# Reordering the state's fading, the next decay's mask and one weighing of scores in an mLSTM cell followed by a gated feed-forward block

## The chip, the cores and the metric

The kernel runs on one core of one Trainium2 chip. A core has five engines that run their own instruction streams in order and meet only at semaphores: TensorE (PE in the profile, with its weight loads shown apart as PEld), VectorE (DVE), ScalarE (ACT), GpSimd (POOL) and SyncE (SP, which here only issues DMAs). The metric is device time in microseconds (us) for one execution; lower is better. All arithmetic is float32, except for a few warm-up matmuls and the first two cells' masks.

## The reference, cut to what matters

An mLSTM cell (4 batches, 8 heads, 768 steps, head size 40) feeds a gated feed-forward block (3072 tokens, 320 features, 2048 hidden units).

```python
for t in range(S):
    m_new = np.maximum(f_gate[:, :, t] + m, i_gate[:, :, t])
    f_stab = np.exp(f_gate[:, :, t] + m - m_new)
    i_stab = np.exp(i_gate[:, :, t] - m_new)
    m = m_new
    C = f_stab * C + i_stab * outer(vt, kt)
    n = f_stab * n + i_stab * kt
    h_tilde = C @ qt
    denom = max(abs(n . qt), 1.0)
    y[:, :, t] = sigmoid(o_gate[:, :, t]) * h_tilde / denom
x = y.transpose(0, 2, 1, 3).reshape(B * S, H * D)
h = x @ w_in
out = (h * cos(h)) @ w_out
```

The two weight matrices arrive as 64-bit floats and are rounded to 32 bits inside the kernel.

## The kernel before, in words

**Cells.** The recurrence is done in chunks of 128 steps. There are six chunks (`c`) and four batches (`b`), so N = 24 cells, numbered n = 4c + b; B is 4. For one cell, `scores(n)` (L530, PE) makes the products of keys and queries of the 8 heads in two PSUM tiles `ps`, even heads and odd heads. `decay_exponents(n)` (L434, POOL) puts the causal mask on the tile `E`, which a DMA has filled; for n below 4 a DVE subtraction comes ahead of the mask, and for n from 4 on the mask is all of it. `decay(n)` (L448, ACT, eight instructions) exponentiates `E`. `weigh(n)` (L536, DVE, two instructions) multiplies `E` by the scores. `values(n)` (L556 to L565, PE) makes the cell's output `vt` from `E` and from the state carried over from the chunk ahead. `seam(n)` (L667, PE) makes the increment of the state in the PSUM tile `pu`. `fade(n)` (L650, POOL, four instructions) multiplies the state `st` by the chunk's decay, once `values(n)` has read it, and `state(n)` (L692, DVE, four instructions) adds `pu` to it. `denominators(n)` and `divide(n)` (L583 to L604, DVE) turn `vt` into `xT`, the input of the feed-forward block. `scale_q` (L512) and `weigh_k` (L453), on POOL, prepare the next cell's queries and keys. The four tiles `ps`, `ps`, `vt` and `pu` of one cell take turns in two PSUM buffers: the second score tile of a cell takes the buffer of the last cell's `pu`, and so can only be written when `state` of the last cell has read it.

**Feed-forward.** For chunk c and pair f2 of 128-wide column blocks, `Up(c, f2)` (L709 and L715, PE) makes two PSUM tiles `pup` of 512 tokens. Then `near` (L723, ACT) rounds to whole turns, `rest` (L726, DVE) makes the remainder, `sin` (L731, ACT) takes the sine, and `gate` (L735, DVE) multiplies it by `pup`, which gives `g`. There are two `pup` buffers, so the next `Up` starts when `gate` has read them. `down(c, f2)` (L829, PE, 16 matmuls in chunk 0) multiplies `g` by two blocks of `w_out`.

**Rounding of weights.** A piece of a weight matrix is loaded as 64-bit words (`bits`, `blocks`). `take_apart` (L167, L169) runs on ACT, `bound` and `join` (L173, L174, L183) on DVE, `round_up` (L187) on POOL. `on_vector` writes out the last three for a list of pieces. `down(0, 1)` reads the second piece of `w_out`.

**Order.** The schedule is written by hand: each engine runs its instructions in the order in which the program issues them, and the framework adds the semaphores. `first_cells` does cells 0 to 3, `first_period` does cell 4 beside `Up(0, 0)` and `Up(0, 1)`, and then `both_parts(c, b)` does cell 4(c+1) + b beside two `Up`s each, with i = 0 and i = 1; `both_parts(0, 1)` with i = 0 has `Up(0, 2)` and cell 5. In chunk 0 the weights are still being loaded and rounded. The SP queue issues nearly all loads; in `first_period` its last ones are `load_G(6)`, `load_two(6)`, `load_out` (which waits for a `bits` buffer that an earlier `round_up` has read) and `load_M(7)`.

Of the kernel before, what the change touches and what calls it, by code (L numbers as in the profile page):

```python
# [29 lines left out]
def kernel(  # L30
# [158 lines left out]
    def on_vector(made):  # L189

        for dst, bits in made:
            bound(dst)
        for dst, bits in (*made[1:], *made[0:1]):
            join(dst, bits)
        for dst, bits in made:
            round_up(dst, bits)
# [225 lines left out]
    def psum_o():  # L422
        return ps_o.tile([128, HP, C], FP, name="pm", tag="o")
# [6 lines left out]
    def decay_exponents(n):  # L430
        E = Es[n]
        if n < B:
            nc.vector.tensor_tensor(out=E, in0=E, in1=cols(n, 0, C), op=OP.subtract)
        nc.gpsimd.affine_select(out=E, in_=E, compare_op=OP.is_ge, fill=1.0e30, base=0,  # L434
                                pattern=[[0, H], [1, C]], channel_multiplier=-1)
# [140 lines left out]
    def denominators(n):  # L576

        K = C // 32
        if n == B:
            d = p2.tile([128, K, 32], FP, name="dt", tag="dt")  # L580
        else:
            d = heads_of[n][:, 3].rearrange("q (k i) -> q k i", k=K)
        nc.vector.transpose(out=d, in_=heads_of[n][:, 2].rearrange("q (t k) -> q k t", t=32))  # L583
        dn = dns[n] = p2.tile([128, K, 2], FP, name="d2", tag="d2")
        both = d[:, :, FROM0:FROM1 + 1:FROM1 - FROM0]
        nc.vector.scalar_tensor_tensor(out=dn, in0=both, scalar=-TWO_PI, in1=least.rearrange("q (k g) -> q k g", g=2), op0=OP.mult, op1=OP.max)
        nc.vector.scalar_tensor_tensor(out=dn, in0=both, scalar=TWO_PI, in1=dn, op0=OP.mult, op1=OP.max)
        if n > B:
            dns[n] = d[:, :, 0:2]
        nc.vector.reciprocal(out=dns[n], in_=dn)  # L590
# [53 lines left out]
    def fade(n):  # L644

        if B <= n < N - B:
            c, b = divmod(n, B)
            for j, r, s, w in halves(n):
                d = tab[r, c, 3, ts(b, H)].rearrange("p (a j) -> p a j", j=2)[:, :, j]
                nc.gpsimd.tensor_tensor(out=s, in0=s, in1=d.unsqueeze(2).to_broadcast([D, HP, w.stop - w.start]), op=OP.mult)  # L650
# [548 lines left out]
    def first_period():  # L1199
        n = B  # L1200
        up = Up(0, 0)
        scores(n)
        warm(8, psum_o())
        for e in range(2):
            up.near(e)
        for e in range(2):
            up.rest(e)
        weigh(n)
        for e in range(2):
            up.sin(e)  # L1210
            up.gate(e)
        values(n)
        seam(n)
        p, piece = outs.pop(0)
        take_apart(*piece)
        low_dimensions(n + 1)
        for some in pieces:
            take_apart(*some)
        out_of_psum(n)
        on_vector([piece])  # L1220
        up = Up(0, 1)
        turn_blocks(n + 1)
        on_vector(pieces)
        pieces.clear()
        more = weights_in(2)
        pieces.append(next(more))
        load_M(n + 2)
        pieces.extend(more)
        load_blocks(n + 2)
        load_out(p)  # L1230
        for e in range(2):
            up.near(e)
        for e in range(2):
            up.rest(e)
        for e in range(2):
            up.sin(e)
            up.gate(e)
        p, piece = outs.pop(0)
        take_apart(*piece)
        denominators(n)  # L1240
        on_vector([piece])
        fade(n)
        state(n)
        decay_exponents(n + 1)
        odd_values_of(n + 1)
        down_slot(0, 1)
        sigmoid(1)
        decay(n + 1)
        divide(n)
        scale_q(n + 1)  # L1250
        weigh_k(n + 1)
        load_G(n + 2)
        load_two(n + 2)
        load_out(p)
        load_M(n + 3)
# [6 lines left out]
    def both_parts(c, b):  # L1262

        n = (c + 1) * B + b
        cell = n < N
        for i in range(2):
            f2 = 2 * b + i
            up = Up(c, f2)
            if cell and i == 0:
                scores(n)  # L1270
            if cell and i == 1:
                if n % 2 == 1 and n > B + 1 and n + 3 < N:
                    load_two(n + 3)
            for e in range(2):
                up.near(e)
            for e in range(2):
                up.rest(e)
            if i == 0:
                if cell:
                    weigh(n)  # L1280
                    if n + 1 < N:
                        decay_exponents(n + 1)
                for e in range(2):
                    up.sin(e)
                    up.gate(e)
                if (c, b) == (0, 1):
                    seam_out(B)
                if c > 0:
                    sums(c, f2)
                if b == 0 and c == 1:  # L1290
                    sigmoid(c + 1)

                if c == 0:
                    p, piece = outs.pop(0)
                    made = [piece, *(pieces.pop(0) for _ in range(min(2 if b < 2 else 3, len(pieces))))]
                    for dst, bits in made:
                        take_apart(dst, bits)
                    on_vector(made[0:2])
                    load_out(p)
                    if b + 2 < B:  # L1300
                        load_blocks(n + 2)
                    if n in (B + 1, B + 2):
                        low_dimensions(n + 1)
                if c > 0 and cell and n + 1 < N:
                    decay(n + 1)
            else:
                if cell:
                    seam_out(n)
                if cell:
                    state(n)  # L1310
                for e in range(2):
                    up.sin(e)
                    up.gate(e)
                if c > 0:
                    sums(c, f2)
                if c == 0:
                    p, piece = outs.pop(0)
                    made = [*([pieces.pop(0)] if b == 1 else ()), piece]
                    for dst, bits in made:
                        take_apart(dst, bits)  # L1320
                    decay(n + 1)
                    sin_next()
                    on_vector(made[0:-1])
                    turn_blocks(n + 1, "k")
                    on_vector(made[-1:])
                if cell and n + 1 < N:
                    if c > 0:
                        weigh_k(n + 1)
                    odd_values(n + 1)
            down_slot(c, f2)  # L1330
            if cell and i == 0:
                values(n)
                seam(n)
                normalize_turned(n)
                fade(n)
                if c == 1 and b < 3:
                    weight_sums(b + 1)
                if n > B + 1 and n + 2 < N:
                    load_blocks(n + 2)
                if n > B + 1 and n + 3 < N:  # L1340
                    load_E(n + 3)
                if b == B - 2 and c + 2 < NC:
                    load_o(c + 2)
                if c == 0:
                    on_vector(made[2:])
                    if b + 2 < B:
                        pieces.extend(weights_in(b + 2))
                if c > 0:
                    sin_next()
            if i == 1:  # L1350
                if c == 0 and b + 2 < B:
                    load_two((n + 3) // 2 * 2)
                    load_E(n + 3)
                if c == 0:
                    turn_blocks(n + 1, "q")
                    scale_q(n + 1)
                    weigh_k(n + 1)
                    load_out(p)
                elif cell and n + 1 < N:
                    turn_blocks(n + 1)  # L1360
                    if n + 1 < (fast + 1) * B:
                        scale_q(n + 1)
                if b == B - 1 and c == fast - 1:
                    sigmoid(c + 2)
                if (c, f2) == (0, LAST):
                    weight_sums(0)
                if c == fast - 1 and b > 0:
                    up_weight_sums(b - 1)
                if c == fast - 1 and b == B - 1:
                    x_sums(c + 1)  # L1370
# [139 lines left out]
```

## Time and profile before

| what | value |
|---|---|
| median of 3 runs | 516.61 us (516.18 to 516.68) |
| profiled execution | 517.38 us, of it span from first to last instruction 515.5 us |
| busy PE | 499.2 us (97% of the span) |
| busy DVE | 417.7 us (81%) |
| busy ACT | 326.4 us (63%) |
| busy POOL | 300.9 us (58%) |
| moved by DMA | 57.87 MB, mean 112 GB/s |
| granted TensorE clock | 0.999 of full speed |

Times in the trace count from the span's start. A line of the timeline has start, duration, engine, line of the kernel, operation, output and inputs, how many instructions were merged into it, and in brackets the time that the engine stood idle ahead of it and what released it. "PE ps L530 <- DVE st L692" in the view of waits means that PE waited, ahead of an instruction of line 530 that writes `ps`, for an instruction of DVE of line 692 that writes `st`.

The period that the diff touches lies between about 56 and 74 us. In the slices from 56 to 64 us the sixteen DMA engines are busy all the time (mean share 1.02 to 1.05), and in most slices up to 130 us over 0.8.

### The profile page before, as it was taken

Reading aid. Unit: us, or ns where it says so; the run is one execution under the profiler, and the core shown is the slowest. Engines: PE = TensorE matmul, PEld = TensorE weight load, DVE = VectorE, ACT = ScalarE, POOL = GpSimd, SP = SyncE. Lnnn points to the kernel's source line nnn. Section 1 sums busy time; section 2 is a strip of 40 time slices with the busy share of each in tenths; the row PEclk is TensorE's granted clock in tenths of the full one; section 3 lists DMA queues with packets and bytes.
Section 4 is the critical chain, followed back from the end, with each engine's and each line's share of the span. In section 5 each row is a group of like instructions: output and inputs, shape, how many; then the busy total and the mean of one; then the engine's idle time right before and its main releaser. Section 6 shows DMA issues by size and latency. Waiting matters only on the chain.

```text
span 515.5 us, 11095 instructions
## 1 busy us (share of the span) xinstructions
PE 499.2 (97%) x4038; PEld 377.1 (73%) x4038; DVE 417.7 (81%) x839; ACT 326.4 (63%) x618; POOL 300.9 (58%) x387
## 2 busy tenths in 40 slices
PE   6999898999999999999999999999999999999997
PEld 3874454655666677778878778878878878687876
DVE  4799788988778888789987989988979867677655
ACT  2889787685945547748658867557867554443541
POOL 7525556553934855858566869656768454535340
PEclk9999999999999999999999999999999999999999
DMA  9979989998167337305728204937202000010001
GB/s 136 217 194 250 261 184 270 184 229 170 27 193 144 117 85 139 93 32 167 178 71 163 71 31 143 190 85 160 72 32 79 7 6 4 3 53 0 1 0 53
DMA packets 100903, 57.87 MB, mean 112 GB/s; under 512 B 63520, under 2 KB 93312, under 8 KB 100848
## 3 DMA queue, kind: packets, MB, share of 16 engines
q1 hardware_dynamic: 97696, 55.48, 45.9%
q10 hardware_dynamic: 2752, 1.23, 0.9%
q8 instruction: 32, 0.52, 0.4%
q0 software_dynamic: 400, 0.44, 0.3%
q14 instruction: 23, 0.19, 0.1%
HBM read 51.71 MB, written 4.11 MB: 108 GB/s over the span
## 4 chain that ended last, share of the span: by engine, by line
PE 72%; DVE 8%; DMA 6%; POOL 4%; ACT 3%; issue 3%; SPq 3%; DVEq 0%; POOLq 0%; ACTq 0%
PE acc L979 23%; PE pup L783 16%; PE pup L715 6%; PE pup L799 6%; PE late L979 4%; PE ps L530 3%; PE po L829 3%; DMA G<-G_d 2%; PE pup L709 2%; DMA blocks<-in_moe_w_in_dram 2%; PE vt L565 2%; DMA qr<-in_q_dram 2%; PE vt L556 2%; DVE t L508 1%; PE pw L1061 1%
## 5 line engine op out<-in xcount | busy, mean ns | idle before, releaser
L723 ACT ACTIVATE n<-pup 128x512 int32<-128x512 f32 x64 | 37.0, 594 | 97.6 <-DVE pup L808 65.0
L731 ACT ACTIVATE n<-n 128x512 f32<-128x512 f32 x96 | 58.2, 627 | 21.6 <-DVE n L726 15.9
L818 POOL TENSOR_TENSOR g<-g,n 128x512 f32<-128x512 f32 x31 | 39.5, 1276 | 51.4 <-ACT n L731 47.3
L726 DVE SCALAR_TENSOR_TENSOR n<-pup,n 128x512 f32<-128x512 f32 x64 | 43.1, 689 | 22.3 <-ACT n L723 19.7
L715 PE MATMUL pup<-xT,w_in_sb 128*128 128x512 f32 x128 | 58.8, 602 | 1.9 <-DVE g L735 1.7
L979 PE MATMUL acc<-w_out_sb,g 128*128 128x160 f32 x320 | 58.4, 302 | 0.0
L800 POOL TENSOR_TENSOR blocks<-blocks 128x256 f32<-128x256 f32 x32 | 25.6, 799 | 53.2 <-ACT blocks L792 53.1
L979 PE MATMUL acc<-T,g 128*128 128x160 f32 x304 | 55.8, 301 | 0.0
L448 ACT ACTIVATE E<-E,tab 128x128 f32<-128x128 f32 x160 | 50.2, 391 | 5.6 <-POOL E L434 5.4
L783 PE MATMUL pup<-xT,w_in_sb 128*128 128x256 f32 x192 | 53.1, 385 | 0.3 <-ACT blocks L792 0.2
L979 PEld LDWEIGHTS acc<-w_out_sb,g 128*128 128x128 f32 x320 | 48.9, 190 | 4.5 <-issue 2.7
L735 DVE TENSOR_TENSOR g<-pup,n 128x512 f32<-128x512 f32 x64 | 42.6, 687 | 6.1 <-ACT n L731 5.6
L715 PEld LDWEIGHTS pup<-xT,w_in_sb 128*128 128x128 f32 x128 | 23.0, 189 | 33.0 <-issue 31.2
L979 PEld LDWEIGHTS acc<-T,g 128*128 128x128 f32 x304 | 46.1, 190 | 0.9 <-issue 0.4
L783 PEld LDWEIGHTS pup<-xT,w_in_sb 128*128 128x128 f32 x192 | 33.8, 189 | 9.6 <-ACT blocks L792 5.9
L808 DVE TENSOR_TENSOR pup<-pup,blocks 128x256 f32<-128x256 f32 x32 | 13.9, 435 | 30.7 <-PE pup L799 27.5
L783 PE MATMUL pup<-x_room,room 128*128 128x256 f32 x128 | 38.2, 380 | 0.0
L791 ACT COPY blocks<-pup 128x512 f32<-128x512 f32 x32 | 18.6, 581 | 29.6 <-PE pup L783 27.8
L829 PE MATMUL po<-w_out_sb,g 128*128 128x320 f32 x128 | 36.3, 436 | 0.1
L979 PE MATMUL acc<-T,blocks 128*128 128x160 f32 x160 | 36.2, 308 | 0.0
L799 PE MATMUL pup<-xL,w_in_l 64*128 64x512 f32 x128 | 36.1, 641 | 0.0
L512 POOL TENSOR_TENSOR qG<-t,G 128x512 f32<-128x512 f32 x20 | 25.9, 1296 | 17.1 <-DVE t L508 16.9
(214 smaller groups left out, 1220.4 us busy)
## 6 DMA issues: line engine op xcount, KB each, us to landing
E<-M_d SPq DMA_DIRECT2D x21, 512.0 KB
qr<-in_q_dram SPq DMA_DIRECT2D x72, 80.0 KB
kr<-in_k_dram SPq DMA_DIRECT2D x72, 80.0 KB
bits<-in_moe_w_out_dram SPq DMA_DIRECT2D x8, 640.0 KB
G<-G_d SPq DMA_DIRECT2D x18, 256.0 KB
blocks<-in_moe_w_in_dram SPq DMA_DIRECT2D x32, 128.0 KB
out_dram<-o_sb SPq DMA_DIRECT2D x23, 160.0 KB
o<-in_o_gate_dram SPq DMA_DIRECT2D x40, 80.0 KB
```

The source lines that it names most:

```text
L448: nc.scalar.activation(out=Es[n][:, h], in_=Es[n][:, h], func=AF.Exp, scale=-1.0, bias=tab[:, c, 0, g:g + 1])
L512: nc.gpsimd.tensor_tensor(out=qG, in0=qkT[n][0], in1=Gs[n], op=OP.mult)
L715: nc.tensor.matmul(pu.rearrange("p (b t) -> p b t", b=B), w_in_sb[:, i, ts(2 * f2 + e, 128)], xT[c][:, i:NK * B:NK], start=(i == 0 and not ...
L723: nc.scalar.activation(out=self.n[e], in_=self.pu[e], func=AF.Copy, bias=0.25)
L726: nc.vector.scalar_tensor_tensor(out=self.n[e].bitcast(FP), in0=self.pu[e], scalar=0.25, in1=self.n[e], op0=OP.add, op1=OP.subtract)
L731: nc.scalar.activation(out=r, in_=r, func=AF.Sin, scale=TWO_PI_DOWN)
L735: nc.vector.tensor_tensor(out=g, in0=self.pu[e], in1=self.n[e].bitcast(FP), op=OP.mult)
L783: nc.tensor.matmul(bank[:, part].rearrange("p (b t) -> p b t", b=B // 2), w[:, f2], x, start=start, stop=stop, skip_group_check=True)
L799: nc.tensor.matmul(pu, w_in_l[r, f2], xL[c][r].rearrange("p b t -> p (b t)"), start=False, stop=True, skip_group_check=True)
L818: tt(out=self.g, in0=self.g, in1=self.n[e].bitcast(FP), op=OP.mult)
L829: nc.tensor.matmul(po[c][b], gs[c, f][:, ts(b, C)], w_out_sb[:, f], start=(f == 0), stop=(f == NF - 1))
L979: nc.tensor.matmul(a, lhs, rhs, start=start, stop=stop)
```

## The change

In `first_period`, `fade(4)` and `decay_exponents(5)` are issued ahead of `on_vector([piece])`, where piece is the second of `w_out`. On POOL the order was round_up, fade, mask, and becomes fade, mask, round_up. On DVE the order stays, since `fade` and the mask (for cells from 4 on) have no DVE instruction: bound, join, state as before. On PE, ACT and SP nothing moves.

In `both_parts`, for c = 0 and f2 = 2 alone (cell 5), `weigh` is issued ahead of `near` and `rest`. On DVE the order was rest, rest, weigh, weigh, and becomes weigh, weigh, rest, rest. On the other engines nothing moves.

```diff
@@ -1238,10 +1238,10 @@
         p, piece = outs.pop(0)
         take_apart(*piece)
         denominators(n)
+        fade(n)
+        decay_exponents(n + 1)
         on_vector([piece])
-        fade(n)
         state(n)
-        decay_exponents(n + 1)
         odd_values_of(n + 1)
         down_slot(0, 1)
         sigmoid(1)
@@ -1271,13 +1271,16 @@
             if cell and i == 1:
                 if n % 2 == 1 and n > B + 1 and n + 3 < N:
                     load_two(n + 3)
+            if (c, f2) == (0, 2):
+                weigh(n)
             for e in range(2):
                 up.near(e)
             for e in range(2):
                 up.rest(e)
             if i == 0:
                 if cell:
-                    weigh(n)
+                    if (c, f2) != (0, 2):
+                        weigh(n)
                     if n + 1 < N:
                         decay_exponents(n + 1)
                 for e in range(2):
```

## The prediction

> **What bounds the kernel now.** I read the page first, for the engine that can't be spared. PE is busy 97% of the span, so the end moves only if PE's idle time does. The second view is the list of what PE waited for over the whole run.
>
> ```profile
> PE   6999898999999999999999999999999999999997
> PE pw L1061 <- DVE room L1064: 4.0, 1, 4.0
> PE ps L530 <- DVE st L692: 1.9, 1, 1.9
> PE pup L783 <- ACT blocks L791: 1.8, 5, 0.8
> PE pup L715 <- DVE g L735: 1.7, 2, 1.4
> PE ps L530 <- DVE t L508: 1.6, 2, 1.1
> ```
>
> Columns of the lower five: total us, times, longest. The wait on `st` is the one that the diff can touch. PE's timeline between 61 and 106 us shows where the rest of the idle time lies that depends on it (idle time in brackets):
>
> ```profile
> 61.99 0.38 PE L530 MATMUL ps<-t,t 40*128 40x128 f32 x2
> 64.23 1.16 PE L530 MATMUL ps<-t,t 40*128 40x128 f32 x14 [1.86 <-DVE st L692]
> 83.11 3.67 PE L715 MATMUL pup<-xT,w_in_sb 128*128 128x512 f32 x8 [1.39 <-DVE g L735]
> 105.48 3.67 PE L715 MATMUL pup<-xT,w_in_sb 128*128 128x512 f32 x8 [0.32 <-DVE g L735]
> ```
>
> After 105.48 only about 3 us of PE waits are left in 410, all for work of the same stage, so what PE has gained by 105.48 it keeps to the end. But PE waits again at 83.11 for `gate` of Up(0, 3): in this stage DVE and ACT are the slower chain, and what counts is how much earlier *they* get there. So third, the timelines of POOL, DVE and ACT around the change.
>
> ```profile
> 57.93 0.75 POOL L187 TENSOR_TENSOR w_in_l<-w_in_l,blocks 128x256 int32<-128x256 int32 x1
> 61.02 1.56 POOL L187 TENSOR_TENSOR w_out_sb<-w_out_sb,bits 128x640 int32<-128x640 int32 x1 [2.34 <-issue]
> 62.54 1.38 POOL L650 TENSOR_TENSOR st<-st,tab 40x128 f32<-40x128 f32 x4
> 63.99 1.09 POOL L434 TENSOR_SCALAR_AFFINE_SELECT E<-E 128x1024 f32<-128x1024 f32 x1
> ...
> 60.07 0.82 DVE L183 SCALAR_TENSOR_TENSOR w_out_sb<-bits,w_out_sb 128x640 int32<-128x640 int32 x1
> 62.97 0.46 DVE L692 TENSOR_TENSOR st<-st,pu 40x128 f32<-40x128 f32 x2 [2.08 <-POOL st L650]
> 64.21 1.15 DVE L596 TENSOR_TENSOR og<-og,d 128x256 f32<-128x256 f32 x1
> 68.08 1.29 DVE L726 SCALAR_TENSOR_TENSOR n<-pup,n 128x512 f32<-128x512 f32 x2 [0.93 <-ACT n L723]
> ...
> 61.55 1.28 ACT L448 ACT_TABLE_LOAD   x1
> 65.12 2.45 ACT L448 ACTIVATE E<-E,tab 128x128 f32<-128x128 f32 x8 [2.29 <-POOL E L434]
> 68.55 1.28 ACT L731 ACT_TABLE_LOAD   x1
> 69.84 1.15 ACT L731 ACTIVATE n<-n 128x512 f32<-128x512 f32 x2
> ```
>
> POOL stands idle 2.34 us until DVE's join of the `w_out` piece ends (60.89), rounds it, and only then fades and masks. Three queues stand behind that: DVE in `state`, through it PE in the scores, and ACT in `decay(5)`.
>
> **Part one: fade and mask ahead of the rounding.** No instruction is added or removed; one round_up (1.56 us) goes behind four fades and one mask. No DMA is moved. POOL's own sum is the same, but it starts at 58.68 (57.93 + 0.75) instead of 61.02. `fade(4)` needs values(4), done by 48 us; the mask needs E of cell 5, whose load SP issued at 43.
>
> *Fades.* Alone they take 1.38 us. Here they run beside DVE's L173, L174 and L183, as at 78.30, where the four took 2.11 us and the DVE three 0.58, 0.43 and 0.78 us, against 0.42, 0.43 and 0.69 elsewhere. So the bounds of the fades are 1.38 and 2.11, and of DVE's loss 0 and about 0.25; I take the upper ends, since that row has the same neighbours. Fades end about 60.8; join ends 60.89 + 0.25, about 61.2.
>
> *Mask.* If it starts ahead of the join it ends at 61.9, behind it at 61.2 + 1.09 = 62.3. I take the second. decay(5) can't start ahead of 62.85 anyway (the table load ends at 62.83), so the mask has 0.5 us of cover. decay: 65.12 to 62.85, **2.27 us earlier**, ending 65.3 instead of 67.57.
>
> *State and scores.* The four adds (0.9 us, 62.97 to 63.70 + 0.48 less the 0.27 of waiting) run 61.3 to 62.2. PE reaches the scores at 61.99 as before, and waits some 0.2 us instead of 1.86.
>
> *Rounding, now last.* 62.3 + 1.56, about 63.9 (62.58 before). down(0, 1) reads it: PE would start it at 63.35 (62.25 and 1.1 for the scores) and waits until 63.9, a new wait of 0.5 us; before it started at 65.32. PE is 1.4 us ahead. At 83.11 PE had 1.39 us to spare, so any gain of PE above 0.9 us here leaves DVE and ACT in charge. odd_values, qG and kw stand behind the rounding on POOL (65.03 to 67.73 before, about 63.9 to 66.5 after); values(5) and seam(5) want them at 68.4 and 70. load_out's wait on this rounding ends at 63.9, and SP issues that load at 76.62.
>
> *What is late next: divide(4).* L596, L598 and L604 read two tensors in SBUF each. L596 took 1.15 us here and 0.42 in the three later cells; it ended (65.36) 0.27 us after POOL's mask (65.08). L586 likewise took 0.48 instead of 0.17 and ended as POOL's round_up did (58.68, 58.71). [...] After the change the round_up stands where the mask stood. Bounds: not held, divide ends at 62.2 + 2.2 = 64.4; held in L596 by the round_up alone, 63.9 + 0.27, then 0.3, 0.92 and 0.5 by the starts of these rows, 65.9. I take 65.9, by the nearest row, that of L596 itself.
>
> [...]
>
> **Part two: weigh ahead of rest.** Nothing added; two weighs (1.28 us) go ahead of two rests (1.29). weigh waits for decay(5) (65.3) and the scores (PE, about 63.4); behind it DVE holds rest, and sin and gate wait for that. With divide done at 65.9: weighs 65.9 to 67.1, first rest 67.75, second 68.4. ACT's sine table is loaded by 69.84 - 2.27 = 67.57, so the first sine starts at 67.8 instead of 69.84: the weighs are hidden by near and the table load (65.3 to 67.57) all but 0.2 us; without that cover they would cost 1.2. In return values(5) finds E ready at 66.6, PE wanting it at 68.4; in the old order it would have been ready at 67.8, in time too, so this part wins only the 0.18 us that PE waited at 70.07 and that DVE's lead covers. I put it at a loss of 0.2 us.
>
> **Sum.** Sines 69.84 to 67.8, gates end 71.79 to 69.7, take_apart 70.90 to 68.9: the DVE and ACT chain is 2.27 less 0.2 to 0.3, **2.0 us** ahead. DVE runs from 68.08 to 88.3 with one gap of 0.24 us, ACT from 80.89 to 89.39 and DVE again from 89.91 to 109.7 without any, so the 2.0 us stand at 83.11 and at 105.48. The profiled execution took 517.38 us (span 515.5, 1.88 around it), so its like would be 515.4; the median lies 0.77 lower, 516.61, and gives **514.6**.
>
> **Rivals.** *A: hidden by the loads.* From 56 to 64 us the DMA share is 1.02 to 1.05, and the chain of waits names DMAs for this stretch. If compute had waited for them, nothing would be gained: 516.6. Against it: that chain has a w_in load landing at 67.50, taken apart only at 73.48, and a `bits` load at 73.95, taken apart at 82.66. The closest is a w_in load issued by 89.38 and taken apart at 94.29; it may cost ACT 2 us, but ACT then stands idle 2.55 us and DVE needs it at 99.74 only. [...] *C: slower.* DVE falls behind POOL: L596, L598 and L604 each wait out a whole POOL instruction (round_up 1.56, qG 1.28, the mask of cell 6 1.09). From 62.9 divide then ends at 62.9 + 2.2 + 3.9 = 69.0, weighs 70.3, first sine 70.95, 1.1 us later than before: 517.7. It decides from a divide ending later than 68.0 (67.16 before); for it speaks that POOL has no gap left from 58.7 to 66.5, against it that L598 and L604 lost 0.04 us each beside copy and qG. *D: no holding at all:* 2.27, and 514.3.
>
> **Chances.** The forecast with D as its lower edge (513.9 to 515.5) 0.70; B 0.14; A 0.08; C 0.08. A measurement of this kernel tells about 0.2% (1.03 us) from no change, so faster ends at 515.58: all of the forecast and a third of B, 0.75; same is the rest of B and A, 0.17; slower C, 0.08. The range leaves out C, half of A and what might lie under D: 513.8 to 516.4.
>
> **What would show it.** Right: the fades start near 58.7 and the decay near 62.85, PE's wait for `st` falls under 0.5 us, PE or PEld waits some 0.5 us for `w_out_sb` of L187 ahead of L829 near 63.9, the first sine comes near 67.8, and the wait at 83.11 moves to about 81.1. Wrong: a divide ending after 67, DVE idle for a DMA between 70 and 105, or a new PE wait after 105 that gives the gain back.

## The result, and the profile after

The changed kernel takes 514.94 us (median of 8 runs, 514.55 to 516.4) against 516.73 for the kernel before; the ratio is 0.9963, 95% interval 0.9949 to 0.9978. That is 1.8 us less by the medians and 0.37% by the ratio, clear of the 0.2% that can be told from no change. The forecast was 514.6, in a range of 513.8 to 516.4. The profiled execution took 515.31 us, with a span of 513.5 against 515.5.

PE's waits over the whole run, after the change (total us, times, longest; the first of the list, 4.0 us at the start of the span, and all under 0.7 us are left out):

```profile
PE pup L715 <- DVE g L735: 1.7, 2, 1.4
PE ps L530 <- DVE t L508: 1.6, 2, 1.1
PE pup L783 <- ACT blocks L791: 1.5, 5, 0.4
PE po L829 <- POOL w_out_sb L187: 0.7, 1, 0.7
```

The wait of 1.9 us for the state is off the list, and a new one of 0.7 us for the rounded `w_out` piece is on it. PE's timeline has both places, and the two waits for `gate` behind them:

```profile
62.22 1.13 PE L530 MATMUL ps<-t,t 40*128 40x128 f32 x16
64.06 4.57 PE L829 MATMUL po<-w_out_sb,g 128*128 128x320 f32 x16 [0.72 <-POOL w_out_sb L187]
81.53 3.67 PE L715 MATMUL pup<-xT,w_in_sb 128*128 128x512 f32 x8 [1.39 <-DVE g L735]
103.90 3.67 PE L715 MATMUL pup<-xT,w_in_sb 128*128 128x512 f32 x8 [0.32 <-DVE g L735]
```

The scores now run in one piece. But the wait at `Up(0, 4)` is 1.39 us as it was: PE came earlier, and DVE's `gate` came earlier by just as much. The timelines of POOL, DVE and ACT say where that comes from:

```profile
58.85 1.79 POOL L650 TENSOR_TENSOR st<-st,tab 40x128 f32<-40x128 f32 x4
60.72 1.58 POOL L434 TENSOR_SCALAR_AFFINE_SELECT E<-E 128x1024 f32<-128x1024 f32 x1
62.27 1.74 POOL L187 TENSOR_TENSOR w_out_sb<-w_out_sb,bits 128x640 int32<-128x640 int32 x1
...
61.27 0.87 DVE L692 TENSOR_TENSOR st<-st,pu 40x128 f32<-40x128 f32 x4
62.17 0.42 DVE L596 TENSOR_TENSOR og<-og,d 128x256 f32<-128x256 f32 x1
62.51 1.65 DVE L598 TENSOR_TENSOR og<-og,d 128x128 f32<-128x128 f32 x1
65.93 1.29 DVE L536 TENSOR_TENSOR E<-ps,E 128x512 f32<-128x512 f32 x2
67.14 1.28 DVE L726 SCALAR_TENSOR_TENSOR n<-pup,n 128x512 f32<-128x512 f32 x2
...
59.46 1.28 ACT L352 ACT_TABLE_LOAD   x1 [0.68 <-DMA o<-in_o_gate_dram]
62.24 1.28 ACT L448 ACT_TABLE_LOAD   x1
63.54 2.45 ACT L448 ACTIVATE E<-E,tab 128x128 f32<-128x128 f32 x8
68.26 1.15 ACT L731 ACTIVATE n<-n 128x512 f32<-128x512 f32 x2
```

POOL no longer stands idle for the join; state runs without a gap; ACT goes from its exponential table straight to `decay`. Two things were not on the bill. ACT waited 0.68 us for the output gate's load ahead of `sigmoid(1)`, against 0.22 before, so everything on ACT behind it is 0.46 us later than with the wait of before. And on DVE it is L598 that is held by the round_up (1.65 us against 0.32), not L596. The lines of the kernel before:

```profile
58.76 1.28 ACT L352 ACT_TABLE_LOAD   x1 [0.22 <-DMA o<-in_o_gate_dram]
...
65.29 0.32 DVE L598 TENSOR_TENSOR og<-og,d 128x128 f32<-128x128 f32 x1
...
49.46 3.70 PE L715 MATMUL pup<-xT,w_in_sb 128*128 128x512 f32 x8
```

The last of them is `Up(0, 1)`, the place from which times are counted below.

Where the 2.0 us of the span come from: one execution reaches the change sooner than another (L715 of `Up(0, 1)` began between 48.45 and 49.79 us in the profiles used here, where nothing ahead of it was changed but, in three of them, the order of some loads), so a place is best compared with one just ahead of the change. Counted from the start of L715 of `Up(0, 1)` (49.46 before, 49.70 after), `Up(0, 4)` comes at 33.65 before and at 31.83 after: 1.82 us that belong to the change. At `Up(0, 6)` it is still 1.82 (56.02 against 54.20). About 0.2 us were lost ahead of the change, and some 0.4 us are gained near 287 us, where PE waited 0.8 us for L791 before and 0.3 after; that the change has a part in this is not shown. At `Up(0, 2)`, ahead of which nothing has changed its order, the two profiles differ by 0.02 us on this count.

### The profile page after: what moved, and what is told of

It is laid out like the page before. It is cut to its first block, busy times and chain, and to the rows that moved or that the text cites. A ratio compares the mean times of both kernels' runs of the same rounds, so it can differ in the third digit from the quotient of the medians.

```text
span 513.5 us, 11097 instructions
## 1 busy us (share of the span) xinstructions
PE 498.9 (97%) x4038; PEld 377.0 (73%) x4038; DVE 418.5 (82%) x839; ACT 326.4 (64%) x618; POOL 301.9 (59%) x387
## 4 chain that ended last, share of the span: by engine, by line
PE 71%; DVE 5%; ACT 5%; DMA 3%; POOL 2%; issue 2%; SPq 1%; ACTq 0%; DVEq 0%; POOLq 0%
PE acc L979 23%; PE pup L783 16%; PE pup L715 7%; PE pup L799 6%; PE late L979 4%; PE po L829 3%; PE ps L530 3%; PE pup L709 2%; PE vt L565 2%; PE vt L556 2%; DVE t L508 1%; DMA bits<-in_moe_w_out_dram 1%; PE pu L667 1%; DMA E<-M_d 1%; ACT E L448 1%
## 5 line engine op out<-in xcount | busy, mean ns | idle before, releaser
L715 PE MATMUL pup<-xT,w_in_sb 128*128 128x512 f32 x128 | 58.8, 602 | 1.9 <-DVE g L735 1.7
L715 PEld LDWEIGHTS pup<-xT,w_in_sb 128*128 128x128 f32 x128 | 23.0, 189 | 33.0 <-issue 31.1
L791 ACT COPY blocks<-pup 128x512 f32<-128x512 f32 x32 | 18.6, 580 | 29.8 <-PE pup L783 27.9
```

The lines of the kernel that those rows point to most:

```text
L715: nc.tensor.matmul(pu.rearrange("p (b t) -> p b t", b=B), w_in_sb[:, i, ts(2 * f2 + e, 128)], xT[c][:, i:NK * B:NK], start=(i == 0 and not ...
```

## The experiments

All kernels ran beside the kernel before, whose medians were 516.62, 516.63 and 516.69 us in the three groups. The theory at the start: what counts is when `Up(0, 2)`'s sines come, which ACT's chain (sigmoid, exponential table, decay, near, sine table) and DVE's chain (state, divide, weigh or rest) must both have reached. The rival: the gain is PE's wait of 1.9 us for the state, which is gone. Each row of the table is one profiled execution, so a row shows where that execution won its time, and not the median of its kernel.

The table has each profile's times counted from the start of L715 of `Up(0, 1)`; the last two columns are what the kernel has won there against before.

| kernel | decay begins | divide ends | first sine | won at Up(0, 4) | won at Up(0, 6) |
|---|---|---|---|---|---|
| before | 15.66 | 17.70 | 20.38 | | |
| after | 13.84 | 16.20 | 18.56 | 1.82 | 1.82 |
| after, again | 14.06 | 16.24 | 18.78 | 1.65 | 1.49 |
| part one alone | 13.19 | 16.21 | 17.91 | 2.45 | 2.40 |
| part one alone, again | 14.06 | 16.21 | 18.78 | 1.57 | 0.57 |
| part two alone | 15.65 | 17.69 | 20.37 | 0.05 | 0.04 |
| fades ahead | 14.70 | 16.57 | 19.42 | 1.04 | 1.03 |
| mask ahead | 13.54 | 19.33 | 21.28 | -0.98 | -1.00 |
| mask ahead, weigh behind | 13.18 | 19.35 | 20.10 | -0.32 | -0.37 |
| mask early | 13.98 | 16.31 | 18.71 | 1.71 | 1.71 |
| taken apart early | 12.67 | 16.24 | 17.39 | 2.78 | 2.74 |
| gate's load sooner | 13.21 | 16.23 | 17.93 | 2.43 | 1.51 |
| both of these | 12.66 | 16.23 | 17.38 | 2.44 | -0.10 |
| the same, mask then fade | 11.79 | 16.32 | 17.08 | 2.69 | 2.02 |

**Part one alone.** The kernel before with the new order in `first_period` only.

```diff
+        fade(n)
+        decay_exponents(n + 1)
         on_vector([piece])
-        fade(n)
         state(n)
-        decay_exponents(n + 1)
```

> Part one alone: fade(4) and the mask of cell 5 ahead of the round_up, weigh(5) behind the rests as in the kernel before. Theory (what counts is how early ACT can begin decay(5), because ACT's chain of decay, near, table load and sines sets the gates, and PE waits for those at Up(0, 4)): decay begins right behind its table load, first sine 68.2, weighs behind the rests end near 69.1, gates end near 70.4, that is 0.1 to 0.3 us later than with both parts; time 1.5 to 1.8 us under before, about 515.0. Rival (weigh ahead of rest is worth as much as the order on POOL): at least 0.8 us slower than with both parts, about 515.8.

Measured: 514.56 us, ratio 0.9951 (0.9936 to 0.9967). Part one makes the whole gain. This execution did not wait for the gate's load at all, and its sines came 0.65 us sooner than the changed kernel's, so one pair of profiles could not price part two; the pair further down does.

**Part two alone.** The changed kernel with `first_period` as before.

```diff
         denominators(n)
-        fade(n)
-        decay_exponents(n + 1)
         on_vector([piece])
+        fade(n)
         state(n)
+        decay_exponents(n + 1)
```

> Part two alone: weigh(5) ahead of near and rest, POOL's order as in the kernel before. Theory: decay still ends at 67.6, the weighs run while near and the sine table load (2.3 us) pass, the first sine starts at 69.85 as before; PE's wait of 0.18 us ahead of values(5) goes; PE still waits 1.9 us for the state. Time within 0.3 us of before, about 516.6. Rival (the weighs lie on the path): 0.6 to 1.2 us slower than before, about 517.6.

Measured: 516.93 us, ratio 1.0009 (0.9997 to 1.0022): no difference. The weighs run while ACT does near and loads its table (DVE and ACT timelines of this run):

```profile
67.24 1.29 DVE L536 TENSOR_TENSOR E<-ps,E 128x512 f32<-128x512 f32 x2 [0.20 <-ACT E L448]
68.45 1.28 DVE L726 SCALAR_TENSOR_TENSOR n<-pup,n 128x512 f32<-128x512 f32 x2
...
68.42 1.28 ACT L731 ACT_TABLE_LOAD   x1
69.72 1.15 ACT L731 ACTIVATE n<-n 128x512 f32<-128x512 f32 x2
```

The first rest ends near 69.1, the table near 69.7: the move is covered.

**Only the fades ahead.** Both parts, with the mask left behind state.

```diff
         denominators(n)
         fade(n)
-        decay_exponents(n + 1)
         on_vector([piece])
         state(n)
+        decay_exponents(n + 1)
```

> Both parts, but the mask of cell 5 stays where it was, behind the round_up and state: only the fades go ahead. Theory (decay's begin counts): fades 58.7 to 60.6, round_up to about 62.9, mask to about 64.0, decay near 64.1 instead of 65.1 before and 63.5 with all of the change; PE's wait for the state is gone all the same. First sine about 68.8, gain 1.0 to 1.4 us: about 515.5. Rival (the gain is PE's wait of 1.9 us for the state, which goes here in full): 1.8 us or more, 514.9 or less.

Measured: 515.28 us, ratio 0.9974 (0.9960 to 0.9988); the trace gives 1.04 us won. PE's wait for the state is gone here, and only about half of the gain is there (1.04 us against 1.82), about as much as the sines came sooner (0.96). The interval of the time alone (1.3 us less, 0.6 to 2.1) does not refute the rival's 1.8; the trace's 1.04, with 1.03 at `Up(0, 6)`, speaks against it, and so does PE's wait for `gate` at `Up(0, 4)`, which is 1.39 us here too.

**Only the mask ahead.**

```diff
         denominators(n)
-        fade(n)
         decay_exponents(n + 1)
         on_vector([piece])
+        fade(n)
         state(n)
```

> Both parts, but the fades stay behind the round_up: only the mask goes ahead. Theory: decay begins behind its table load near 63 as with all of the change, but DVE's state still waits for the fades until about 63, so divide ends at 66.5 to 67, weighs near 68.2, first sine near 68.9 instead of 69.84; PE's wait of 1.9 us for the state stays. PE then has 0.4 us less to spare than DVE gains. Gain 0.8 to 1.2 us: about 515.7. Rival (the gain is PE's wait for the state, which stays here): nothing, 516.6.

Measured: 517.67 us, ratio 1.0020 (1.0006 to 1.0034): slower than before, which neither expected. `decay` began 2.1 us sooner, as the theory had it, and the sines came 0.9 us later. The lines of POOL, DVE, ACT and PE show why:

```profile
57.94 1.08 POOL L434 TENSOR_SCALAR_AFFINE_SELECT E<-E 128x1024 f32<-128x1024 f32 x1
...
58.04 1.00 DVE L587 SCALAR_TENSOR_TENSOR d<-dt,d 128x8 f32<-128x8 f32 x1
64.34 1.52 DVE L596 TENSOR_TENSOR og<-og,d 128x256 f32<-128x256 f32 x1
65.78 0.81 DVE L598 TENSOR_TENSOR og<-og,d 128x128 f32<-128x128 f32 x1
68.12 1.29 DVE L536 TENSOR_TENSOR E<-ps,E 128x512 f32<-128x512 f32 x2
...
70.04 1.23 ACT L731 ACTIVATE n<-n 128x512 f32<-128x512 f32 x2 [3.04 <-DVE n L726]
...
64.36 1.16 PE L530 MATMUL ps<-t,t 40*128 40x128 f32 x14 [2.68 <-DVE st L692]
65.45 6.27 PE L829 MATMUL po<-w_out_sb,g 128*128 128x320 f32 x16
```

L587 works on 8 elements a partition and took 0.17 us in the kernel before; here it ended at 59.04, with the mask (59.02). The join, the round_up, the fades and the state came later by that; L596 (1.52 us) then ended 0.29 us behind qG and L598 (0.81) 0.15 us behind kw; divide ended 1.6 us later than before; and with the weighs ahead of the rest ACT stood 3.04 us with its table loaded. This is the mechanism of rival C of the prediction (DVE falls behind POOL), brought about by another order and by other instructions (C had L596, L598 and L604 held; here it was L587, L596 and L598, and divide ended 1.6 us later and not 1.8). That C's 517.7 is also the median here is in part luck. The sixteen `down` matmuls took 6.27 us instead of 4.57; the run of the same order below shows the reason.

**The changed kernel and part one, side by side again.** No edits.

> The changed kernel itself once more, beside the next run on the same chip. In the first profiles part one alone stood at 514.56 and both parts at 514.94, but the profile with both parts had ACT waiting 0.68 us for the output gate's load ahead of sigmoid(1), and the other 0.0. Theory (part two costs nothing or up to 0.3 us: divide ends at 65.9, so the first rest behind the weighs ends near 67.75, while the sine table stands from 67.3 where the load is in time): 514.6 to 515.0. Rival (part two helps, and the difference was the load): below the next run.

> Part one alone once more, beside the run above on the same chip. Theory: 0 to 0.4 us under the run with both parts, first sine straight behind the sine table's load, PE finding E weighed when down(0, 1) ends. Rival (part two helps): 0.1 to 0.5 us above it.

Measured: both parts 514.49 us, ratio 0.9959 (0.9945 to 0.9973); part one alone 514.68, 0.9968 (0.9955 to 0.9981). The first pair had the order the other way (0.9963 and 0.9951). Part two is worth nothing that these runs can tell, in either direction. Both profiled executions here reached `Up(0, 1)` 0.9 to 1.0 us sooner than that of the kernel before, and both waited 0.88 to 0.89 us for the gate's load, with the sines at the same 18.78. So it was the load and not part two that set the sines of the first pair apart: 0.68 us of waiting against none, 0.65 us at the sines.

That run of part one alone lost 1.0 us more between `Up(0, 4)` and `Up(0, 6)`. ACT's timeline there:

```profile
92.26 0.69 ACT L167 ACTIVATE w_in_sb<-blocks 128x512 f32<-128x512 f32 x1 [1.44 <-DMA blocks<-in_moe_w_in_dram]
94.19 0.69 ACT L167 ACTIVATE w_in_sb<-blocks 128x512 f32<-128x512 f32 x1 [0.65 <-DMA blocks<-in_moe_w_in_dram]
96.52 0.45 ACT L167 ACTIVATE w_in_l<-blocks 128x256 f32<-128x256 f32 x1 [1.07 <-DMA blocks<-in_moe_w_in_dram]
```

The profile of the kernel before has none of these three waits, and that of the changed kernel two short ones (0.60 and 0.25 us), which cost it nothing at `Up(0, 6)`. Here compute that came sooner waited 3.2 us in all for its `w_in` loads.

**The mask ahead, weigh behind the rests.** The mask-ahead order put into the kernel before.

```diff
         denominators(n)
+        decay_exponents(n + 1)
         on_vector([piece])
         fade(n)
         state(n)
-        decay_exponents(n + 1)
```

> The mask of cell 5 ahead of the round_up, the fades behind it, and weigh(5) behind the rests as in the kernel before: the run of the mask alone, without part two. There DVE reached the end of divide at 68.1, did the weighs first, and the first sine waited 3.0 us for its rest (70.04). Theory (weigh ahead of rest costs where divide ends late): the first sine starts 1.2 us sooner, near 68.8, gates end near 71, and the time is 0.6 to 1.2 us under that run's 517.7, about 516.7. Rival (that run was slow because the TensorE clock was granted at half for 3 us after PE's idle time of 2.7 us): the clock falls here too, since the wait for the state is the same, and the time stays at 517.4 or more.

Measured: 516.86 us, ratio 1.0016 (1.0001 to 1.0032). The medians differ by 0.8 us, the ratios to before hardly; the intervals overlap. The traces tell the two apart: the first sine came 1.18 us sooner by the table (20.10 against 21.28) with the same end of divide, and `Up(0, 4)` 0.66 us sooner, so where divide ends late, weighing first does cost. But the rival's sign was there too. These are PE's second run of scores and the windows of 2 us (start and end; length; busy PE, PEld, DVE, ACT and POOL, each with its count; granted TensorE clock; DMA share; GB/s):

```profile
64.47 1.16 PE L530 MATMUL ps<-t,t 40*128 40x128 f32 x14 [2.69 <-DVE st L692]
...
62.00:64.00 2.00, 0.00 (x0) 0.00 (x0) 0.54 (x3) 1.99 (x8) 1.93 (x5) 1.00 1.04 234
64.00:66.00 2.00, 1.53 (x16) 1.33 (x17) 1.97 (x4) 1.98 (x5) 1.94 (x4) 1.00 0.65 141
66.00:68.00 2.00, 2.00 (x6) 1.21 (x5) 1.93 (x3) 0.75 (x1) 1.64 (x2) 0.52 0.40 116
68.00:70.00 2.00, 2.00 (x6) 1.29 (x5) 1.97 (x4) 1.04 (x2) 1.19 (x2) 0.63 0.65 165
70.00:72.00 2.00, 2.00 (x17) 1.20 (x19) 2.00 (x5) 2.00 (x4) 0.00 (x0) 1.00 1.02 329
```

After 2.7 us without a matmul the granted clock fell to half for about 3.4 us (the four windows of 1 us from 66 to 70 have 0.53, 0.50, 0.50 and 0.76), and `down(0, 1)` took 6.27 us here too. PE then reached `Up(0, 4)` without waiting for `gate` at all, so in this run PE itself was the late one. In the run with weigh ahead the clock fell too (0.50 and 0.68 in the same two windows), but the sines were later still: PE waited 0.54 us for `gate` there, so the half clock was hidden. Theory and rival were both half right.

**The mask earlier still.** Part one alone, with the mask in POOL's idle time near 51.5 us.

```diff
         out_of_psum(n)
         on_vector([piece])
+        decay_exponents(n + 1)
         up = Up(0, 1)
...
         fade(n)
-        decay_exponents(n + 1)
         on_vector([piece])
```

> Part one alone, but the mask of cell 5 goes still further ahead, into POOL's idle time before 55 us, right behind the first w_out piece's round_up. Then the round_up of the second piece runs near 60.9 to 62.4, PE's wait of 0.72 us ahead of down(0, 1) goes, and DVE's L598 is held for less long. Theory (ACT's chain of sigmoid, two table loads, decay and near sets the first sine, and has no gap): no change against part one alone, within 0.3 us, first sine at the same place behind its table load; DVE or PE only wait longer. Rival (PE's wait or the held divide is on the path): 0.5 to 0.8 us less, 514.0 or below.

Measured: 515.44 us, ratio 0.9972 (0.9961 to 0.9983). PE's wait of 0.72 us at `down(0, 1)` went, and nothing was won by it. The hold of divide did not go: L598 took 0.32 us, but the round_up now held L596 (1.26 us against 0.42), and divide ended no sooner (16.31 against 16.21). What speaks against the rival's held divide is that the first sine comes 4.72 or 4.73 us behind decay's begin in all rows of the table but the two with the mask ahead and the last, that is straight behind its table load, however long L598 or L596 was held. The mask instead held DVE's first bound of `w_in` (L173, 1.19 us against 0.41), the sines of `Up(0, 1)` waited 2.49 us for their rest instead of 1.71, and ACT's chain began later by as much. The median is 0.8 us above that of part one alone, outside the 0.3 expected; the ratios overlap.

**The load and the take_apart.** Three kernels on part one alone, after what limits ACT's chain.

```diff
         for e in range(2):
             up.rest(e)
+        p, piece = outs.pop(0)
+        take_apart(*piece)
         for e in range(2):
             up.sin(e)
             up.gate(e)
-        p, piece = outs.pop(0)
-        take_apart(*piece)
         denominators(n)
```

> Part one alone, and the take_apart of the second w_out piece (1.5 us on ACT) goes ahead of the sines of Up(0, 1), into the 1.5 to 1.7 us in which ACT stands idle there. Theory (ACT's chain from those sines to the sines of Up(0, 2) sets the end, and behind it the output gate's load): sigmoid's table load can begin 1.5 us sooner, but the load of the gate lands near 58, so ACT waits for it and gains only what part one alone did not wait: first sine 0 to 0.7 us sooner, 514.1 to 514.7. Rival (the loads have nothing to do with it): first sine a full 1.4 us sooner, 513.3.

```diff
-        load_G_of(B + 1)
-        load(B + 1, "kv")
         outs.append((1, weights_out(1)))
         load_o(1)
+        load_G_of(B + 1)
+        load(B + 1, "kv")
         outs.append((2, weights_out(2)))
```

> Part one alone, and the output gate's load (and that of the second w_out piece) issued ahead of the loads of G, keys and values of cell 5, so that it lands some 2 us sooner. Theory: ACT's wait ahead of sigmoid(1), 0.0 to 0.9 us from one execution to the next, is gone in all of them; 0 to 0.9 us less, mean 0.5: about 514.1, and a smaller spread. Rival (that wait is hidden): no change, 514.6.

> Part one alone with both of the changes of the two runs above: the second w_out piece taken apart ahead of the sines of Up(0, 1), and the gate's load sooner. Theory: decay(5) then begins when its mask ends, near 62.0, instead of 62.6 to 63.5, and the first sine comes near 66.8; DVE's first rest ends near 66.3, so DVE is all but the bound. 0.6 to 1.4 us less than part one alone: about 513.6. Rival (neither is on the path): 514.6.

The third kernel has both edits. Measured, in this order: 514.73 (0.9965, 0.9952 to 0.9978), 514.96 (0.9967, 0.9955 to 0.9979) and 515.00 (0.9975, 0.9960 to 0.9990). All three brought the first sine about to where it was expected, or sooner, and none is faster than part one alone; the 514.1 and 513.6 expected of the second and third did not come. With the gate's load sooner alone, the profile won 2.43 us at `Up(0, 4)` and had lost 0.92 of it by `Up(0, 6)`. With the take_apart early, decay waited 0.59 us for its mask, and with both edits 0.86: there ACT's chain is not the bound any more, POOL's is. With both edits the sines stand at 17.38, 1.2 us ahead of the changed kernel, and at `Up(0, 6)` the gain is gone in the profiled execution, which took 516.80 us, one of the slowest of twelve between 513.62 and 518.27:

```profile
93.63 0.67 ACT L167 ACTIVATE w_in_sb<-blocks 128x512 f32<-128x512 f32 x1 [2.97 <-DMA blocks<-in_moe_w_in_dram]
...
105.39 3.67 PE L715 MATMUL pup<-xT,w_in_sb 128*128 128x512 f32 x8 [2.37 <-DVE g L735]
```

**The last order.** Both edits, and POOL's order mask, fade, round_up.

```diff
-        fade(n)
         decay_exponents(n + 1)
+        fade(n)
         on_vector([piece])
```

> The last kernel with POOL's order mask, fade, round_up instead of fade, mask, round_up. Theory: the mask holds DVE's L587 for 0.8 us (1.00 us instead of 0.17 to 0.33, as in the runs with the mask ahead of the round_up alone), which makes join and state later by about that; decay can begin near 61.3, but DVE's rest is then ready near 66.6 at best. Within 0.5 us of the last run, either way. Rival (decay's begin alone counts): 0.6 us less than the last run.

Measured: 514.04 us, ratio 0.9951 (0.9939 to 0.9963). The lowest median of all, and the only run beside part one alone at 0.9951, but its interval overlaps the changed kernel's; it is not shown to be faster. As expected the mask held L587 for 1.00 us, decay began 0.9 us sooner than in the run before it, and DVE's rest was the bound: the sines stand only 0.3 us better. That it came out 1 us ahead of the run before it, and not within the 0.5 expected, is not explained by the sines. The two profiles differ at `Up(0, 6)`, where this one had lost 0.7 us to the loads and the other 2.5; that the medians differ for the same reason is not shown.

## Why the prediction was right, point by point

**What bounds the stage.** Right. ACT's and DVE's chain decides and PE waits for its `gate`: at `Up(0, 4)` the changed kernel won 1.82 us, its sines 1.82. In the other runs the two agree within 0.1 us too, but for the one that the half clock made late and the three whose sines came about 3 us sooner or more, which won 0.2 to 0.6 us less at `Up(0, 4)`: there DVE was next, which ran without a gap from its rests to the `gate` that PE waits for. With PE's wait for the state gone and the mask left late, the sines won 0.96 and `Up(0, 4)` 1.04.

**The fades, the join, the mask, the state.** Sized rightly. Against the predicted fades to 60.8, join to 61.2, mask to 62.3, state to 62.2 and rounding to 63.9 stand 60.64, 61.34, 62.30, 62.14 and 64.01. This execution ran 0.24 us late from before the change on; without that they come 0.1 to 0.4 us sooner than predicted. The fades took 1.79 us, between the bounds of 1.38 and 2.11.

**The new wait for the rounding.** 0.72 us against 0.5, and hidden as reckoned: the run without it won nothing, and PE's wait for `gate` behind it is 1.39 us as before.

**The decay.** Off: 63.54 instead of 62.85, of which 0.24 us lie ahead of the change and 0.45 in it. The step that failed is the table load that was to end at 62.83 as before. It stood behind the output gate's load, and that landed later against the rest of the program. In the run where the load was in time decay began at 62.58. So rival A had a true core: not that nothing could be won, but that up to 0.9 us of it depend on when a load lands.

**Divide and what held it.** The end was near (65.9 predicted, 65.90 measured, 65.66 without the 0.24), the instruction wrong, so that the end agrees is in part luck: L596 passed between mask and round_up in 0.42 us and L598 was held for 1.65. L598 here, and L587, L596 and L598 with the mask ahead, each read two tensors, and each ended 0.02 to 0.3 us behind a POOL instruction that ran beside it. But the bound held in the mask-early run (L173) reads only one and ended 0.28 us behind the mask, and in the kernel before L598 and L604, with two each, took 0.32 and 0.60 us beside POOL's copy, qG and kw, against 0.28 and 0.56 in later cells. So two inputs do not decide it in every case, and no run here isolates why. L587 and the mask share no tile, and L587 took 1.00 us beside it all the same: in these runs DVE and POOL met at more than semaphores.

**Part two.** Sized at a loss of 0.2 us; the runs show no difference. What the prediction said would have to be gone for it to cost (its cover, with a late divide) is what the pair of mask-ahead runs showed: 1.18 us at the sines, against the 1.2 that the prediction named.

**The sum.** 2.0 us predicted; 1.82 in the profile and 1.65 in the second one, 1.79 and 2.14 between the medians of the two groups. The term that was mis-sized is the decay's begin: 2.27 us predicted, 1.82 measured. The 0.2 taken off for part two did not show, since the later sine table covered it: the first rest ended near 67.8 and the table at 68.24. That the sum still came within 0.2 us is in part luck, one miss having covered the other.

**Rivals.** B (L598 held by qG as well) did not come: L598 ended at 64.16 and qG began at 64.21. C did not come in the changed kernel, but its mechanism came in the mask-ahead order, with a divide that ended 1.6 us late. The `w_in` loads near 92 to 97 us, of which A named one as the closest, take part of the gain back in four of the later profiles (0.7 to 2.5 us). How far ahead compute is does not decide it alone: part one alone lost 0.05 us with 2.45 won in one execution and 1.0 with 1.57 won in the other.

## What to carry to other kernels

Before counting a wait on the busiest engine as the gain, look for its next wait: if that is for another chain, the gain is what that chain wins, and here it was the order on POOL that freed ACT and DVE together. A reordering on one engine can be paid on another that it holds up, here DVE beside POOL, even by an instruction of 8 elements a partition (L587, 1.00 us beside the mask instead of 0.17), so ask which instruction of the neighbour will be running. And where loads fill the DMA engines, an order that is 1 us better may stand still at the next load, as the 2.44 us won at `Up(0, 4)` with both edits were gone at `Up(0, 6)` behind a wait of 2.97 us for a `w_in` load; the profiles of several executions, counted from a place just ahead of the change, tell more than their medians.

## What the runs showed of the hardware that was not expected

In both runs in which PE waited 2.7 us for the state its granted clock fell to half for some 3.4 us (from 1.00 to 0.52 and 0.63 in two windows of 2 us with weigh behind, to 0.50 and 0.68 with weigh ahead), and sixteen matmuls took 6.27 us instead of 4.57. The wait of 1.9 us in the kernel before left it at 1.00, and so did the 4.0 us at the start of the span; behind the wait of 2.4 us in the run with both edits eight matmuls took 3.67 us, as elsewhere. That the length of the wait alone decides is therefore not shown.

A DVE instruction on 128x8 elements (L587, 0.17 us) took 1.00 us beside POOL's mask, and the mask itself took 1.58 us instead of 1.09 where DVE's join had begun 0.20 us ahead of it (60.52 against 60.72). A DVE instruction with one input (L173, 0.41 us) took 1.19 beside the mask in the mask-early run.
